# Window attention with a gate, one core: scores of four quarters added up in one PSUM bank

## The chip, the core and the metric

The kernel runs on one core of a Trainium2 chip. A core has a matrix engine (TensorE, PE in the profile), a vector engine (VectorE, DVE), a scalar engine (ScalarE, ACT), GpSimd (POOL) and a queue engine (SyncE, SP) which here issues nearly all of the loads. Each engine executes its own instructions in order, and engines wait for each other through semaphores. Matmul results go to PSUM, which has eight banks of 128 partitions by 512 float32 numbers. The metric is the device time of one execution in microseconds (us); lower is better.

## The reference

A single decode step for two sequences. Everything is float32.

```python
xn = _layernorm(x)                                   # x: 2 x 1 x 512
# attention over the last W = 4096 positions of a cache of 32768
q = (xn @ wq)                                        # 32 query heads of 128, 8 key/value heads
k = k_cache[:, :, Sk - W:, :]; v = v_cache[:, :, Sk - W:, :]
p = softmax(einsum("bhqd,bhkd->bhqk", q, k) * Dh ** -0.5)
s = einsum("bhqk,bhkd->bhqd", p, v).reshape(B, 1, 4096) @ wo
# gated MLP on the same xn
z = gelu(xn @ w_in); z1 = z[..., :896]; z2 = _layernorm(z[..., 896:])
y = (z1 * (w_sp * z2 + b_sp)) @ w_out
out = x + s * silu(y)
```

The weights and the two windows of the caches amount to 89.4 MB, each byte of which is read once.

## The kernel before

**Units.** The attention is cut into eight units. A unit holds two key/value heads of one sequence, so eight query heads. Its keys are one load of 4096 KB and its values another: partition p holds 64 consecutive positions of one of the two heads (64 partitions for each head), J = 64 positions of 128 numbers each.

**Loads.** All large tensors pass through a pool `ring` of four slots of 32 KB for each partition. SP issues the loads in one order: `win`, `wout`, two halves of `wq`, then `k0`, `v0`, `k1`, `v1`, ... `k7`, `v7`, then `wo` in pieces of 16, 8, 4, 2, 1 and 1 blocks. The fifth load takes the first slot again, and so on. So the load of `k` of unit u+2 waits on SP until the last reader of `k` of unit u has ended, and the load of `v` of unit u+2 until `values` of unit u has ended.

**Scores.** A unit's 64 positions are done in NCH = 4 quarters of JC = 16 positions. For quarter m:

- `turn(u, m)`: VectorE transposes the 128x2048 block of keys in 32x32 squares into `kt`, of which there are two buffers.
- `shares(u, m)`: four matmuls of 128x32 weights (the queries) and 512 columns, one for each quarter of the 128 numbers of a head, into one PSUM bank `sh`. They give four shares of each score, which lie in different partitions. ScalarE copies the bank to `shs`.
- `add_shares(u, m)`: one matmul with the 0/1 matrix `add_dq` (128x128) adds the four shares. Its output is the m-th of the four banks of the tile `s`. Partition 32g + 16a + 4h of it holds the scores of query h of key head a with the keys of partition group g; the other rows are zero.

**Softmax.** `row_max` takes the maximum over 1536 columns (three banks) and then over 512 columns (the last). `share_max` masks it (`t` twice, `mg`), sums over partitions by a matmul (`mo`), takes a maximum (`mx`) and makes the bias `nb`. `probs` are two exponentials on ScalarE, each over 1024 of the 2048 columns (even and odd ones), which also add up the sums `l`. `probs_t` transposes `p` on VectorE in two halves of 1024 columns into `pT`. `weights` sums `l` over partitions by a matmul and makes the factors `wd` on VectorE.

**Values.** `values` is 16 matmuls of 128x32 weights and 512 columns into the bank `acc`, with four groups of columns of the array side by side. `scale_out` scales `acc` on ScalarE in four pieces into `o`, and `collect` (four matmuls) puts the rows of interest into a bank `col` for each sequence. After the last unit of a sequence `gather` reduces it into `oT`. At the end `part` (56 records) and `so` multiply by `wo`, and two vector operations apply the gate.

**Order.** All the engines' instructions keep the order in which the program writes them (`InOrder`). In one turn of the loop over units, with `prev` the unit before: exponentials of `prev`; turn and shares of quarter 0 of u; both halves of `probs_t` and `weights` of `prev`; `add_shares` 0; `values` of `prev`; then for the quarters 1, 2 and 3 turn, shares, `add_shares`; then `scale_out` and `collect` of `prev`; the maxima of u.

**PSUM.** `s` takes four banks, and `sh`, `acc`, `mo` and `col` one each: all eight.

Of the kernel before, what the change touches and what calls it, by code (L numbers as in the profile page):

```python
# [9 lines left out]
F32 = mybir.dt.float32  # L10
AF = mybir.ActivationFunctionType
ALU = mybir.AluOpType
AX = mybir.AxisListType

P = 128
HQ, DH = 32, 128
G = 4
# [4 lines left out]
def ap(t, offset, dims):  # L22

    return bass.AP(tensor=t.tensor, offset=t.offset + offset, ap=[list(t.ap[0])] + [list(d) for d in dims])
# [18 lines left out]
def kernel(  # L43
# [14 lines left out]
    pe, dve, act, sp = (InOrder(tc, e) for e in (nc.tensor, nc.vector, nc.scalar, nc.sync))  # L58
    B, _, D = x.shape
    _, HKV, SK, _ = k_cache.shape  # L60
    W = min(4096, max(256, SK // 4))
    REP = HQ // HKV
# [7 lines left out]
    J = 2 * W // P  # L70
    JC = 512 // 32
    NCH = J // JC
    SLOT = J * DH

    ring = ctx.enter_context(tc.tile_pool(name="ring", bufs=4))
    cst = ctx.enter_context(tc.tile_pool(name="cst", bufs=1))
    sb = ctx.enter_context(tc.tile_pool(name="sb", bufs=2))
# [5 lines left out]
    def const(name, *shape):  # L83
        return cst.tile([P, *shape], F32, tag=name, name=name)

    def bank(name, tag):
        return ps.tile([P, 512], F32, tag=tag, name=name)


    xs = cst.tile([B, D], F32, tag="xs", name="xs")  # L90
# [8 lines left out]
    wqt = []  # L99
# [29 lines left out]
    nc.gpsimd.memset(hT, 0.0)  # L129
    x4 = const("x4", DC)  # L130
    nc.gpsimd.memset(x4, 0.0)
    add_dq = const("add_dq", G, 32)
    nc.gpsimd.memset(add_dq, 0.0)
    sel = const("sel", 35)
    nc.gpsimd.memset(sel, 0.0)
# [33 lines left out]
    same = const("same", G, 32)  # L169
    dve.tensor_copy(same, ap(rowm, 0, [[0, G], [1, 32]]))  # L170
    same = same.rearrange("p g c -> p (g c)")
    heads = const("heads", 16, 8)
    dve.tensor_copy(heads, ap(rowm, 0, [[0, 16], [4, 8]]))
    heads = heads.rearrange("p x r -> p (x r)")
    diag = const("diag", 4)
    dve.tensor_reduce(diag, rowm.rearrange("p (j r) -> p j r", j=4), axis=AX.X, op=ALU.add)
    dve.tensor_reduce(sel[:, 3:35:4], rowm.rearrange("p (j r) -> p r j", j=4), axis=AX.X, op=ALU.add)
    for a in range(2):
        dve.tensor_copy(add_dq[:, :, 16 * a : 16 * a + 16 : 4], rowm[:, 16 * a : 16 * a + 16].rearrange("p (g h) -> p g h", g=G))
    add_dq = add_dq.rearrange("p g r -> p (g r)")  # L180
    am = const("am", 2)
    dve.tensor_reduce(am, ap(rowm, 0, [[16, 2], [4, REP]]), axis=AX.X, op=ALU.add)
    negm = const("negm", 2)
    dve.tensor_scalar(negm, am, -1.0, BIG, op0=ALU.add, op1=ALU.mult)


    FQ = FH // G
# [56 lines left out]
    for j in range(FT):  # L244
        g = j % G
# [10 lines left out]
    dve.tensor_mul(gate, gate, y)  # L256


    pq = ps.tile([P, 2, 512], F32, tag="s", name="q_ps")
    for k in range(KT):  # L260
        for r in range(2):
            for g in range(G):
                c = (r * G + g) * 512
                pe.matmul(
                    pq[32 * g : 32 * g + 32, r, :], xnT[:, k, :], wqt[k // 2][:, k % 2, c : c + 512],
                    start=(k == 0), stop=(k == KT - 1),
                )
    qT = sb.tile([P, 1024], F32, tag="qT", name="qT", bufs=1)
    dve.transpose(qT, pq.rearrange("p r c -> p (r c)"))
    qm = const("qm", 2 * B * 64)  # L270
    for gs in range(G):
        for b in range(B):
# [16 lines left out]

    def turn(u, m):  # L290

        u.kt[m] = sb.tile([P, JC, DH], F32, tag="kt", name=f"kt{u.n}_{m}")
        dve.transpose(
            u.kt[m].rearrange("p j d -> p (j d)"), u.k[:, JC * m : JC * m + JC, :].rearrange("p j d -> p (j d)")
        )

    def shares(u, m):

        u.sh = bank(f"sh{u.n}_{m}", "sh")
        for dq in range(4):  # L300
            pe.matmul(
                u.sh[32 * dq : 32 * dq + 32, :], q_of(u, dq), u.kt[m][:, :, 32 * dq : 32 * dq + 32],
                start=True, stop=True,
            )
        u.shs[m] = sb.tile([P, 512], F32, tag="shs", name=f"shs{u.n}_{m}")
        act.activation(u.shs[m], u.sh, AF.Copy)

    def add_shares(u, m):
        if m == 0:
            u.s = ps.tile([P, NCH, 512], F32, tag="s", name=f"s{u.n}")  # L310
            u.m4 = sb.tile([P, 2, 2], F32, tag="m4", name=f"m4_{u.n}")
        pe.matmul(u.s[:, m, :], add_dq, u.shs[m], start=True, stop=True)

    def row_max(u, i, c0, c1):
        dve.tensor_reduce(
            u.m4[:, i, :], ap(u.s, 512 * c0, [[1, 2], [2, 256 * (c1 - c0)]]), axis=AX.X, op=ALU.max
        )

    def share_max(u):
        t = sb.tile([P, 2], F32, tag="t", name=f"t{u.n}")  # L320
        dve.tensor_scalar_mul(t, u.m4[:, :, 0], am[:, 0:1])
        dve.scalar_tensor_tensor(t, u.m4[:, :, 1], am[:, 1:2], t, op0=ALU.mult, op1=ALU.add)
        mg = sb.tile([P, 2, G], F32, tag="mg", name=f"mg{u.n}")
        dve.tensor_mul(mg, ap(t, 0, [[1, 2], [0, G]]), ap(grpm, 0, [[0, 2], [1, G]]))
        u.mo = bank(f"mo{u.n}", "mo")
        pe.matmul(u.mo[:, : 2 * G], same, mg.rearrange("p a g -> p (a g)"), start=True, stop=True)
        mx = sb.tile([P, 1], F32, tag="mx", name=f"mx{u.n}")
        dve.reduce_max(mx, u.mo[:, : 2 * G], axis=AX.X)
        u.nb = sb.tile([P, 2], F32, tag="nb", name=f"nb{u.n}")
        dve.scalar_tensor_tensor(u.nb, ap(mx, 0, [[0, 2]]), -SCALE, negm, op0=ALU.mult, op1=ALU.add)  # L330

    def probs(u):

        u.p = sb.tile([P, J, 32], F32, tag="p", name=f"p{u.n}", bufs=1)
        u.l = sb.tile([P, 2], F32, tag="l", name=f"l{u.n}")
        for a in range(2):
            act.activation(
                ap(u.p, a, [[2, J * 16]]), ap(u.s, a, [[2, J * 16]]), AF.Exp,
                bias=u.nb[:, a : a + 1], scale=SCALE, accum_out=u.l[:, a : a + 1],
            )  # L340

    def probs_t(u, half):
        if half == 0:
            u.pT = sb.tile([P, J, 32], F32, tag="pT", name=f"pT{u.n}", bufs=1)
        h = slice(J // 2 * half, J // 2 * (half + 1))
        dve.transpose(u.pT[:, h].rearrange("p j r -> p (j r)"), u.p[:, h].rearrange("p j k -> p (j k)"))

    def weights(u):
        pe.matmul(u.mo[:, 2 * G : 2 * G + 2], heads, u.l, start=True, stop=True)
        l = sb.tile([P, 1], F32, tag="ls", name=f"ls{u.n}")  # L350
        dve.reduce_sum(l, u.mo[:, 2 * G : 2 * G + 2], axis=AX.X)
        dve.reciprocal(l, l)
        u.wd = sb.tile([P, 4], F32, tag="wd", name=f"wd{u.n}")
        dve.tensor_scalar_mul(u.wd, diag, l)

    def values(u):
        u.acc = bank(f"acc{u.n}", "acc")
        NQ = J // 4
        for q in range(NQ):
            c = q % G  # L360
            pe.matmul(
                u.acc[32 * c : 32 * c + 32, :], ap(u.pT, 4 * q * 32, [[4, 32]]),
                u.v[:, 4 * q : 4 * q + 4, :].rearrange("p j d -> p (j d)"), start=(q < G), stop=(q >= NQ - G),
            )

    def scale_out(u):
        u.o = sb.tile([P, 4, DH], F32, tag="o", name=f"o{u.n}")
        for jj in range(4):
            act.activation(
                u.o[:, jj, :], u.acc[:, jj * DH : (jj + 1) * DH], AF.Copy, scale=u.wd[:, jj : jj + 1]  # L370
            )
# [3 lines left out]
    def collect(u):  # L375
        if u.w == 0:
            col[u.b] = bank(f"col{u.b}", "col")[:, : 4 * 32].rearrange("p (j d) -> p j d", j=4)
        for e in range(4):
            pe.matmul(
                col[u.b][32 * u.w : 32 * u.w + 32], sel[:, 3 - e : 35 - e], u.o[:, :, 32 * e : 32 * e + 32],  # L380
                start=(e == 0), stop=(e == 3),
            )
# [28 lines left out]
                for b in range(B):  # L411
                    sp.dma_start(x4[16 * b : P : 32, :], by_group(x, b, 0, DC))

    def finish(u):
        scale_out(u)
        collect(u)

    prev = None
    for u in units:
        if prev is not None:  # L420
            probs(prev)
        turn(u, 0)
        shares(u, 0)
        if prev is not None:
            probs_t(prev, 0)
            probs_t(prev, 1)
            weights(prev)
        add_shares(u, 0)
        if prev is not None:
            values(prev)  # L430
        for m in range(1, NCH):
            turn(u, m)
            shares(u, m)
            add_shares(u, m)
        if prev is not None:
            finish(prev)
        row_max(u, 0, 0, NCH - 1)
        row_max(u, 1, NCH - 1, NCH)
        share_max(u)
        if prev is not None:  # L440
            gather(prev)
        prev = u
    probs(prev)
    probs_t(prev, 0)
    probs_t(prev, 1)
    weights(prev)
    values(prev)
    finish(prev)
    gather(prev)


# [49 lines left out]
```

## Time and profile before

| | us |
|---|---|
| three runs | 260.6, 262.8, 265.55 |
| their median | 262.8 |
| the profiled execution, whole time | 261.21 |
| its span, from the first to the last instruction | 259.4 |

| engine | busy us | share of the span |
|---|---|---|
| TensorE | 161.7 | 62% |
| VectorE | 137.0 | 53% |
| ScalarE | 54.8 | 21% |

The page of the profile shows the busy time of each engine, the span in 40 equal slices (each digit a busy share in tenths), the queues of the transfers, the chain of work that ended last, and the costliest groups of instructions. Nearly all instructions stand under line 37, because a helper records them; the names of tiles tell them apart. A float32 matmul shows as two records, so 16 matmuls are "x32". The granted clock is the share of TensorE's full clock that the chip gave in a stretch. The span and all durations are of one execution; the whole time of that execution is 1.8 us more than its span.

### The profile page before, as it was taken

Reading aid. Unit: us, or ns where it says so; the run is one execution under the profiler, and the core shown is the slowest. Engines: PE = TensorE matmul, PEld = TensorE weight load, DVE = VectorE, ACT = ScalarE, POOL = GpSimd, SP = SyncE. Lnnn points to the kernel's source line nnn. Section 1 sums busy time; section 2 is a strip of 40 time slices with the busy share of each in tenths; the row PEclk is TensorE's granted clock in tenths of the full one; section 3 lists DMA queues with packets and bytes.
Section 4 is the critical chain, followed back from the end, with each engine's and each line's share of the span. In section 5 each row is a group of like instructions: output and inputs, shape, how many; then the busy total and the mean of one; then the engine's idle time right before and its main releaser. Section 6 shows DMA issues by size and latency. Waiting matters only on the chain.

```text
span 259.4 us, 2310 instructions
## 1 busy us (share of the span) xinstructions
PE 161.7 (62%) x898; PEld 49.2 (19%) x898; DVE 137.0 (53%) x191; ACT 54.8 (21%) x109; POOL 2.5 (1%) x13
## 2 busy tenths in 40 slices
PE   0261894285297559637872976497368729763893
PEld 0111221011121122122220212121222112121131
DVE  3234115861893486369618933873696189435000
ACT  4004100011301240233033012401330330123100
POOL 3000000000000000000000000000000000000000
PEclk9996579569569967995998599779959995997798
DMA  7999999999999997999499769958994998591000
GB/s 284 418 466 409 450 428 414 450 429 419 450 424 422 450 419 344 384 424 421 149 414 470 328 237 407 404 248 323 467 419 167 404 424 386 197 396 56 0 3 1
DMA packets 3794, 89.54 MB, mean 345 GB/s; under 512 B 438, under 2 KB 454, under 8 KB 840
## 3 DMA queue, kind: packets, MB, share of 16 engines
q1 hardware_dynamic: 3768, 89.40, 81.6%
q8 instruction: 7, 0.11, 0.2%
q10 hardware_dynamic: 16, 0.01, 0.0%
q14 instruction: 3, 0.02, 0.0%
HBM read 89.40 MB, written 0.00 MB: 345 GB/s over the span
## 4 chain that ended last, share of the span: by engine, by line
PE 53%; DVE 18%; DMA 16%; ACT 9%; issue 3%; ACTq 0%
PE s L37 17%; PE sh L37 16%; PE acc L37 14%; DMA k<-in_A_k_cache_dram 12%; ACT shs L37 7%; DVE m L37 7%; DVE kt L37 7%; DMA win<-in_B_w_in_dram 4%; PE part L37 2%; PE z L37 2%; DVE t L37 1%; PE mo L37 1%; ACT p L37 1%; DVE mg L37 1%; DVE mx L37 1%
## 5 line engine op out<-in xcount | busy, mean ns | idle before, releaser
L37 DVE STREAM_TRANSPOSE kt<-k 128x2048 f32<-128x2048 f32 x32 | 72.8, 2297 | 19.8 <-PE sh L37 19.1
L37 PE MATMUL s<-shs,add_dq 128*128 128x512 f32 x64 | 43.6, 768 | 21.3 <-ACT shs L37 21.3
L37 PE MATMUL sh<-kt,qbd 128*32 128x512 f32 x256 | 41.6, 729 | 24.3 <-DVE kt L37 24.3
L37 ACT ACTIVATE shs<-sh 128x512 f32<-128x512 f32 x32 | 19.1, 597 | 125.2 <-PE sh L37 125.2
L37 DVE TENSOR_REDUCE m<-s 128x2 f32<-128x1536 f32 (+1 forms) x16 | 18.8, 1219 | 42.9 <-PE s L37 42.9
L37 PE MATMUL acc<-v,pT 128*32 128x512 f32 x256 | 35.8, 709 | 0.7 <-DVE pT L37 0.7
L37 ACT ACTIVATE p<-s,nb 128x1024 f32<-128x1024 f32 x16 | 18.5, 1168 | 34.8 <-DVE nb L37 34.8
L37 DVE STREAM_TRANSPOSE pT<-p 128x1024 f32<-128x1024 f32 x16 | 19.0, 1224 | 4.4 <-ACT p L37 4.3
L37 PEld LDWEIGHTS s<-shs,add_dq 128*128 128x128 f32 x64 | 11.1, 218 | 46.2 <-ACT shs L37 43.7
L37 PEld LDWEIGHTS acc<-v,pT 128*32 128x32 f32 x256 | 9.3, 146 | 30.8 <-issue 30.0
L37 PE MATMUL mo<-mg,same 128*128 128x8 f32 x16 | 3.3, 280 | 18.4 <-DVE mg L37 18.4
L37 PEld LDWEIGHTS sh<-kt,qbd 128*32 128x32 f32 x256 | 6.2, 117 | 42.9 <-issue 37.8
L37 ACT ACTIVATE o<-acc,wd 128x128 f32<-128x128 f32 x32 | 9.1, 374 | 7.3 <-PE acc L37 7.3
L37 PE MATMUL q_ps<-wq,xnT 128*32 128x512 f32 x64 | 9.3, 734 | 0.6 <-DMA wq<-in_A_wq_dram 0.6
L37 PE MATMUL col<-o,sel 128*32 128x128 f32 x64 | 8.5, 275 | 1.3 <-ACT o L37 1.3
L37 PEld LDWEIGHTS col<-o,sel 128*32 128x32 f32 x64 | 6.3, 109 | 7.5 <-ACT o L37 6.7
L37 PE MATMUL z<-win,xnT 128*32 128x448 f32 x32 | 4.5, 723 | 4.6 <-DMA win<-in_B_w_in_dram 4.6
L37 PEld LDWEIGHTS mo<-l,heads 128*128 128x128 f32 x16 | 4.0, 311 | 14.6 <-issue 11.6
L37 PEld LDWEIGHTS mo<-mg,same 128*128 128x128 f32 x16 | 2.6, 203 | 21.1 <-DVE mg L37 21.1
L37 PE MATMUL mo<-l,heads 128*128 128x2 f32 x16 | 4.7, 363 | 2.9 <-ACT p L37 2.9
L37 PE MATMUL part<-wo,oT 128*32 128x512 f32 x56 | 6.2, 593 | 0.4 <-issue 0.4
L37 PE MATMUL y<-wout,hT 128*32 128x512 f32 x14 | 3.6, 1059 | 4.0 <-DVE hT L37 4.0
(99 smaller groups left out, 57.3 us busy)
## 6 DMA issues: line engine op xcount, KB each, us to landing
k<-in_A_k_cache_dram SPq DMA_DIRECT2D x8, 4096.0 KB, 21.6
v<-in_A_v_cache_dram SPq DMA_DIRECT2D x8, 4096.0 KB, 13.1
wq<-in_A_wq_dram SPq DMA_DIRECT2D x2, 4096.0 KB, 29.7
wo<-in_A_wo_dram SPq DMA_DIRECT2D x1, 4096.0 KB
win<-in_B_w_in_dram SPq DMA_DIRECT2D x1, 3584.0 KB
wo<-in_A_wo_dram SPq DMA_DIRECT2D x1, 2048.0 KB
wout<-in_B_w_out_dram SPq DMA_DIRECT2D x1, 1792.0 KB, 15.1
wo<-in_A_wo_dram SPq DMA_DIRECT2D x1, 1024.0 KB
```

The lines of the kernel that those rows point to most:

```text
L37: return self.tc.keep_in_program_order(call(*args, **kwargs))
```

## The change

The four quarters of a unit's scores go to one bank instead of four. The 0/1 matrix `add_dq` becomes 131 columns wide; for quarter m the matmul takes the 128 columns that begin at 3 - m, so that quarter m's rows land on rows that the other quarters leave at zero, and the four matmuls accumulate in the bank. Row 4r + m of a group of 32 then belongs to quarter m and to r = 4a + h.

- `row_max` is gone; the maximum `m2` is one reduction over 512 columns, the two masking operations `t` are gone, and `mg` multiplies by a prepared mask `spot`. The sum over partitions is two accumulating matmuls (`same_r`) instead of one.
- The two exponentials take 256 columns each, `probs_t` is one transpose of 512 columns.
- `values` takes its 32 weight columns from one position `j` of `pT` and the positions j, j+16, j+32, j+48 of `v`: 16 matmuls as before.
- PSUM: two banks each for `s`, `sh` and `acc`, one each for `mo` and `col`. `kt` has three buffers, `p` and `pT` two.
- The order in a turn of the loop: exponentials, transpose, weights and `values` of `prev` come first. Then the quarters of u, in which `add_shares` of quarter m - 1 stands behind `shares` of quarter m; `scale_out` of `prev` stands in quarter 1, `collect` of `prev` ahead of the last `add_shares`.
- Some vector operations are added to the set-up (`rowr`, `same_r`, `spot`), and `qT` is transposed in two halves. The loads and their order are the same.

```diff
+    BANKS = {"s": 2, "sh": 2, "acc": 2, "mo": 1, "col": 1}
...
-    add_dq = const("add_dq", G, 32)
+    add_dq = const("add_dq", NCH - 1 + P)
...
+    spot = const("spot", 2, G, NCH)
+    for a in range(2):
+        dve.tensor_mul(spot[:, a], ap(grpm, 0, [[1, G], [0, NCH]]), ap(diag, 0, [[0, G], [1, NCH]]))
+        dve.tensor_scalar_mul(spot[:, a], spot[:, a], am[:, a : a + 1])
...
-    dve.transpose(qT, pq.rearrange("p r c -> p (r c)"))
+    for r in range(2):
+        dve.transpose(qT[:, 512 * r : 512 * r + 512], pq[r])
...
-        pe.matmul(u.s[:, m, :], add_dq, u.shs[m], start=True, stop=True)
+        pe.matmul(u.s, add_dq[:, NCH - 1 - m : NCH - 1 - m + P], u.shs[m], start=(m == 0), stop=(m == NCH - 1))
...
-    def row_max(u, i, c0, c1):
-        dve.tensor_reduce(
-            u.m4[:, i, :], ap(u.s, 512 * c0, [[1, 2], [2, 256 * (c1 - c0)]]), axis=AX.X, op=ALU.max
-        )
...
-        dve.tensor_scalar_mul(t, u.m4[:, :, 0], am[:, 0:1])
-        dve.scalar_tensor_tensor(t, u.m4[:, :, 1], am[:, 1:2], t, op0=ALU.mult, op1=ALU.add)
+        dve.tensor_reduce(m2, ap(u.s, 0, [[1, 2], [2, 256]]), axis=AX.X, op=ALU.max)
...
-        pe.matmul(u.mo[:, : 2 * G], same, mg.rearrange("p a g -> p (a g)"), start=True, stop=True)
+        for a in range(2):
+            pe.matmul(u.mo[:, : G * NCH], same_r, mg[:, a], start=(a == 0), stop=(a == 1))
...
-                ap(u.p, a, [[2, J * 16]]), ap(u.s, a, [[2, J * 16]]), AF.Exp,
+                ap(u.p, a, [[2, 256]]), ap(u.s, a, [[2, 256]]), AF.Exp,
...
-                u.acc[32 * c : 32 * c + 32, :], ap(u.pT, 4 * q * 32, [[4, 32]]),
-                u.v[:, 4 * q : 4 * q + 4, :].rearrange("p j d -> p (j d)"), start=(q < G), stop=(q >= NQ - G),
+                u.acc[32 * c : 32 * c + 32, :], u.pT[:, j, :], u.v[:, j : J : JC, :],
+                start=(j < G), stop=(j >= JC - G),
...
         if prev is not None:
             probs(prev)
-        turn(u, 0)
-        shares(u, 0)
-        if prev is not None:
-            probs_t(prev, 0)
-            probs_t(prev, 1)
+            probs_t(prev)
             weights(prev)
-        add_shares(u, 0)
-        if prev is not None:
             values(prev)
-        for m in range(1, NCH):
+        for m in range(NCH):
             turn(u, m)
             shares(u, m)
-            add_shares(u, m)
+            if m > 0:
+                add_shares(u, m - 1)
+            if m == 1 and prev is not None:
+                scale_out(prev)
         if prev is not None:
-            finish(prev)
-        row_max(u, 0, 0, NCH - 1)
-        row_max(u, 1, NCH - 1, NCH)
+            collect(prev)
+        add_shares(u, NCH - 1)
         share_max(u)
```

More of the change, by code (lines that the diff above doesn't have):

```diff
@@ L86, in bank @@
     def bank(name, tag):
-        return ps.tile([P, 512], F32, tag=tag, name=name)
+        return ps.tile([P, 512], F32, tag=tag, name=name, bufs=BANKS[tag])
     xs = cst.tile([B, D], F32, tag="xs", name="xs")
@@ L171 @@
     same = same.rearrange("p g c -> p (g c)")
[L172 to L177, printed above, removed]
+    rowr = const("rowr", 8)
+    dve.tensor_reduce(rowr, rowm.rearrange("p (r m) -> p r m", m=NCH), axis=AX.X, op=ALU.add)
+    same_r = const("same_r", G, 8, NCH)
+    dve.tensor_copy(same_r, ap(rowr, 0, [[0, G], [1, 8], [0, NCH]]))
+    same_r = same_r.rearrange("p g r m -> p (g r m)")
+    diag = const("diag", NCH)
+    dve.tensor_reduce(diag, rowm.rearrange("p (r m) -> p m r", m=NCH), axis=AX.X, op=ALU.add)
+    dve.tensor_copy(sel[:, 3:35:4], rowr)
     for a in range(2):
-        dve.tensor_copy(add_dq[:, :, 16 * a : 16 * a + 16 : 4], rowm[:, 16 * a : 16 * a + 16].rearrange("p (g h) -> p g h", g=G))
-    add_dq = add_dq.rearrange("p g r -> p (g r)")
+        dve.tensor_copy(
+            ap(add_dq, NCH - 1 + 16 * a, [[32, G], [4, REP]]),
+            rowm[:, 16 * a : 16 * a + 16].rearrange("p (g h) -> p g h", g=G),
+        )
     am = const("am", 2)
-    dve.tensor_reduce(am, ap(rowm, 0, [[16, 2], [4, REP]]), axis=AX.X, op=ALU.add)
+    dve.tensor_reduce(am, rowm.rearrange("p (a x) -> p a x", a=2), axis=AX.X, op=ALU.add)
     negm = const("negm", 2)
     dve.tensor_scalar(negm, am, -1.0, BIG, op0=ALU.add, op1=ALU.mult)
+    spot = const("spot", 2, G, NCH)
+    for a in range(2):
+        dve.tensor_mul(spot[:, a], ap(grpm, 0, [[1, G], [0, NCH]]), ap(diag, 0, [[0, G], [1, NCH]]))
+        dve.tensor_scalar_mul(spot[:, a], spot[:, a], am[:, a : a + 1])
     FQ = FH // G
@@ L256 @@
     dve.tensor_mul(gate, gate, y)
-    pq = ps.tile([P, 2, 512], F32, tag="s", name="q_ps")
+    pq = [bank(f"q_ps{r}", "s") for r in range(2)]
     for k in range(KT):
@@ L264 @@
                 pe.matmul(
-                    pq[32 * g : 32 * g + 32, r, :], xnT[:, k, :], wqt[k // 2][:, k % 2, c : c + 512],
+                    pq[r][32 * g : 32 * g + 32, :], xnT[:, k, :], wqt[k // 2][:, k % 2, c : c + 512],
                     start=(k == 0), stop=(k == KT - 1),
@@ L290, in turn @@
     def turn(u, m):
-        u.kt[m] = sb.tile([P, JC, DH], F32, tag="kt", name=f"kt{u.n}_{m}")
+        u.kt[m] = sb.tile([P, JC, DH], F32, tag="kt", name=f"kt{u.n}_{m}", bufs=3)
         dve.transpose(
@@ L309, in add_shares @@
         if m == 0:
-            u.s = ps.tile([P, NCH, 512], F32, tag="s", name=f"s{u.n}")
-            u.m4 = sb.tile([P, 2, 2], F32, tag="m4", name=f"m4_{u.n}")
-        pe.matmul(u.s[:, m, :], add_dq, u.shs[m], start=True, stop=True)
-    def row_max(u, i, c0, c1):
-        dve.tensor_reduce(
-            u.m4[:, i, :], ap(u.s, 512 * c0, [[1, 2], [2, 256 * (c1 - c0)]]), axis=AX.X, op=ALU.max
-        )
-    def share_max(u):
-        t = sb.tile([P, 2], F32, tag="t", name=f"t{u.n}")
-        dve.tensor_scalar_mul(t, u.m4[:, :, 0], am[:, 0:1])
-        dve.scalar_tensor_tensor(t, u.m4[:, :, 1], am[:, 1:2], t, op0=ALU.mult, op1=ALU.add)
-        mg = sb.tile([P, 2, G], F32, tag="mg", name=f"mg{u.n}")
-        dve.tensor_mul(mg, ap(t, 0, [[1, 2], [0, G]]), ap(grpm, 0, [[0, 2], [1, G]]))
+            u.s = bank(f"s{u.n}", "s")
+        pe.matmul(u.s, add_dq[:, NCH - 1 - m : NCH - 1 - m + P], u.shs[m], start=(m == 0), stop=(m == NCH - 1))
+    def share_max(u):
+        m2 = sb.tile([P, 2], F32, tag="m2", name=f"m2_{u.n}")
+        dve.tensor_reduce(m2, ap(u.s, 0, [[1, 2], [2, 256]]), axis=AX.X, op=ALU.max)
+        mg = sb.tile([P, 2, G * NCH], F32, tag="mg", name=f"mg{u.n}")
+        dve.tensor_mul(mg, ap(m2, 0, [[1, 2], [0, G * NCH]]), spot.rearrange("p a g m -> p a (g m)"))
         u.mo = bank(f"mo{u.n}", "mo")
-        pe.matmul(u.mo[:, : 2 * G], same, mg.rearrange("p a g -> p (a g)"), start=True, stop=True)
+        for a in range(2):
+            pe.matmul(u.mo[:, : G * NCH], same_r, mg[:, a], start=(a == 0), stop=(a == 1))
         mx = sb.tile([P, 1], F32, tag="mx", name=f"mx{u.n}")
-        dve.reduce_max(mx, u.mo[:, : 2 * G], axis=AX.X)
+        dve.reduce_max(mx, u.mo[:, : G * NCH], axis=AX.X)
         u.nb = sb.tile([P, 2], F32, tag="nb", name=f"nb{u.n}")
@@ L332, in probs @@
     def probs(u):
-        u.p = sb.tile([P, J, 32], F32, tag="p", name=f"p{u.n}", bufs=1)
+        u.p = sb.tile([P, 512], F32, tag="p", name=f"p{u.n}")
         u.l = sb.tile([P, 2], F32, tag="l", name=f"l{u.n}")
@@ L337, in probs, with probs_t @@
             act.activation(
-                ap(u.p, a, [[2, J * 16]]), ap(u.s, a, [[2, J * 16]]), AF.Exp,
+                ap(u.p, a, [[2, 256]]), ap(u.s, a, [[2, 256]]), AF.Exp,
                 bias=u.nb[:, a : a + 1], scale=SCALE, accum_out=u.l[:, a : a + 1],
             )
[L342 to L346, printed above, removed]
+    def probs_t(u):
+        u.pT = sb.tile([P, JC, 32], F32, tag="pT", name=f"pT{u.n}")
+        dve.transpose(u.pT.rearrange("p j r -> p (j r)"), u.p)
     def weights(u):
-        pe.matmul(u.mo[:, 2 * G : 2 * G + 2], heads, u.l, start=True, stop=True)
+        pe.matmul(u.mo[:, 32:34], same_r, u.l, start=True, stop=True)
         l = sb.tile([P, 1], F32, tag="ls", name=f"ls{u.n}")
-        dve.reduce_sum(l, u.mo[:, 2 * G : 2 * G + 2], axis=AX.X)
+        dve.reduce_sum(l, u.mo[:, 32:34], axis=AX.X)
         dve.reciprocal(l, l)
-        u.wd = sb.tile([P, 4], F32, tag="wd", name=f"wd{u.n}")
+        u.wd = sb.tile([P, NCH], F32, tag="wd", name=f"wd{u.n}")
         dve.tensor_scalar_mul(u.wd, diag, l)
@@ L357, in values @@
         u.acc = bank(f"acc{u.n}", "acc")
-        NQ = J // 4
-        for q in range(NQ):
-            c = q % G
+        for j in range(JC):
+            c = j % G
             pe.matmul(
-                u.acc[32 * c : 32 * c + 32, :], ap(u.pT, 4 * q * 32, [[4, 32]]),
-                u.v[:, 4 * q : 4 * q + 4, :].rearrange("p j d -> p (j d)"), start=(q < G), stop=(q >= NQ - G),
+                u.acc[32 * c : 32 * c + 32, :], u.pT[:, j, :], u.v[:, j : J : JC, :],
+                start=(j < G), stop=(j >= JC - G),
             )
@@ L412 @@
                     sp.dma_start(x4[16 * b : P : 32, :], by_group(x, b, 0, DC))
-    def finish(u):
-        scale_out(u)
-        collect(u)
     prev = None
@@ L443 @@
     probs(prev)
-    probs_t(prev, 0)
-    probs_t(prev, 1)
+    probs_t(prev)
     weights(prev)
     values(prev)
-    finish(prev)
+    scale_out(prev)
+    collect(prev)
     gather(prev)
```

## The prediction, made blind

> **What bounds the kernel now.** I read the page first: the span and the row of the transfers in 40 slices.
>
> ```profile
> span 259.4 us, 2310 instructions
> DMA  7999999999999997999499769958994998591000
> ```
>
> The transfers are at nine tenths or more up to the 15th slice, with one exception at the start, and from the 16th on there are holes. So the first 97 us are set by the memory, and later something makes the transfers wait. Next came busy time by stretches: start and end, length, busy time of PE, weight loads, DVE, ACT and POOL, then the granted clock, the transfers' share and GB/s.
>
> ```profile
> 2.00:97.00 95.00, 51.26 (x267) 14.93 (x268) 46.62 (x89) 18.72 (x33) 1.01 (x3) 0.80 1.00 429
> 115.00:235.00 120.00, 81.87 (x422) 24.71 (x422) 76.06 (x83) 29.08 (x60) 0.00 (x0) 0.86 0.83 347
> 122.00:124.00 2.00, 2.00 (x9) 0.41 (x12) 2.00 (x2) 0.00 (x0) 0.00 (x0) 0.50 1.14 492
> 124.00:126.00 2.00, 2.00 (x24) 0.60 (x20) 1.53 (x1) 0.00 (x0) 0.00 (x0) 0.98 0.04 8
> 126.00:128.00 2.00, 1.87 (x20) 0.37 (x12) 0.05 (x1) 0.00 (x0) 0.00 (x0) 1.00 0.00 0
> ```
>
> With its queue full, the core takes 429 GB/s; in the second half the mean is 347, because in each unit there are some 4 us without a byte, as from 124 to 128. Who holds the transfers back is in the waits of SP's queue (total us, times, longest):
>
> ```profile
> SPq L37 <- PE acc L37: 139.7, 7, 20.3
> ```
>
> SP stands up to 20.3 us ahead of a load of `v` until `values` has given the slot back, and the load of `k` is queued behind it. Compute is the bound of the later units. Its period is in the chain of work (start, us, what):
>
> ```profile
> 115.64 2.23 DVE kt L37
> 117.88 0.14 issue
> 118.01 1.97 PE sh L37 x8
> 120.06 0.61 ACT shs L37
> 120.71 2.08 PE s L37 x2
> 122.79 4.23 PE acc L37 x32
> ...
> 132.68 1.04 PE sh L37 x8
> 133.81 0.61 ACT shs L37
> 134.46 1.14 PE s L37 x2
> 135.62 2.37 DVE m L37 x2
> 138.01 0.24 DVE t L37
> 138.28 0.23 DVE t L37
> 138.53 0.18 DVE mg L37
> 138.75 0.40 PE mo L37 x2
> 139.18 0.18 DVE mx L37
> 139.38 0.16 DVE nb L37
> 139.54 2.23 DVE kt L37
> ```
>
> From one bias `nb` to the next it is 139.54 - 115.64 = 23.90 us, and every engine waits in turn: each quarter goes through shares, copy and sum without anything beside it, and the maxima come at the end. Matmuls begin at half the clock (`sh` 1.97 against 1.04, `s` 2.08 against 1.14) and run at the full one from about 124 on.
>
> **The loads as the new floor.** The loads themselves are not changed.
>
> ```profile
> k<-in_A_k_cache_dram SPq DMA_DIRECT2D x8, 4096.0 KB, 21.6
> 16.74 30.25 DMA k<-in_A_k_cache_dram
> ```
>
> A load is 4096 KB = 4.194 MB, so a unit's two are 8.39 MB, at 429 GB/s 19.55 us. The first `k` lands at 16.74 + 30.25 = 46.99. If the queue never runs dry, the eighth lands 7 x 19.55 later, at 183.8. [...]
>
> Does the queue stay full? It takes slots in order. The load of `k` for unit u+2 waits for the last turn of unit u, some 9 us after `k` of u landed, and its own time in the queue comes after three more loads, 29 us after that landing. The load of `v` for u+2 waits for `values` of u, worked out below at 24 us after the landing at most, against 39. Some 15 us of slack are left, so nothing that SP waits for is late.
>
> **Compute, part by part.** Durations for the remaining terms:
>
> ```profile
> 121.03 4.50 DVE L37 STREAM_TRANSPOSE kt<-k 128x2048 f32<-128x2048 f32 x2
> L37 DVE TENSOR_REDUCE m<-s 128x2 f32<-128x512 f32 x8 | 5.4, 680 | 0.0
> ```
>
> ```profile
> 235.23 2.37 ACT p L37 x4
> 237.62 1.26 DVE pT L37
> 238.93 5.97 PE acc L37 x32
> 244.92 1.15 ACT o L37 x4
> 246.12 1.06 PE col L37 x8
> 247.18 0.43 issue
> 247.61 6.25 PE part L37 x56
> ```
>
> ```profile
> 241.50 0.19 PEld L37 LDWEIGHTS acc<-v,pT 128*32 128x32 f32 x4 [0.66 <-issue]
> 242.35 0.19 PEld L37 LDWEIGHTS acc<-v,pT 128*32 128x32 f32 x4 [0.66 <-issue]
> ```
>
> Turns: two back to back take 4.50, so four take 9.0, and with the third `kt` buffer nothing stops them: the fourth needs only `shares` of quarter 0. With 0.14 for the issue and a few hundredths to start, `sh` of quarter 3 can begin 9.2 us after `k` lands. Matmuls from there: the new order puts `sh` 3, `s` 2, `col`, `s` 3 on PE, 1.04 + 1.14 + 1.06 + 1.14 = 4.4; the copies of 0.61 lie beside them. That cover needs the two `sh` banks; without it each copy costs its 0.61. The three earlier `sh` and two `s` fit into the turns when `values` is done in time.
>
> Maximum: from the end of the last `s` (134.46 + 1.14 = 135.60) to the start of the next work (139.54) was 3.94. The reduction goes from 2.37 to 0.70 (the 680 ns row and a hand-over), the two `t` go (138.01 to 138.53, 0.52), the second `mo` matmul adds between 0 and 0.40; I take 0.3, since the two follow each other without a wait. That leaves 2.05. So `nb` comes 9.2 + 4.4 + 2.05 = 15.6 after the landing.
>
> Exponentials and transpose: 2.37 for two of 1024 columns. For two of 256 the ends are a quarter, 0.59, and two copies of 512 columns, 2 x 0.61 = 1.22; I take 1.05, near the upper end, since a copy or a reduction of few elements still costs 0.16 to 0.18 here. Half of `pT` took 1.26 and a turn of twice its columns 2.23 to 2.25, so 512 columns take about 0.76. Together 1.8. `weights` lies beside `values`.
>
> `values`: the same 16 matmuls, 4.23 when mostly warm. Cold, four records pass each 0.85 us (241.50 to 242.35), so 32 take 6.8. I see no reason for another price in the strided columns of `v`; if there were one, it would stand under the turns of the next unit, as long as `sh` 0 isn't late by more than some 2 us.
>
> Set-up: the added vector operations come before the wait for `win` at 12 us, where DVE has nothing else; without that they would be 1 us.
>
> Compute alone would have the period 1.8 + `values` 4.2 to 6.8 + four `sh`, four `s` and `col` (4 x 1.04 + 4 x 1.14 + 1.06 = 9.8) + 2.05 = 17.8 to 20.4 us, about 19 in the middle. That is under the 19.55 of the loads, though not by much. So the bound moves from the round of the engines to the loads, and what each unit saves is 23.9 - 19.55 = 4.35 us, not the 6 that compute alone gives.
>
> **Sum.** The last `k` lands at 183.8; `nb` at 199.4; `values` begins at 201.2; from there to the end nothing is changed: before, 238.93 to 259.4, 20.5 us. Span 221.7. Are the last weights there? `v7` and 8.39 MB of `wo` take 29.3 us after 183.8, so the last block lands at 213.1; `part` would begin at 201.2 + 8.7 = 209.9 and need its last four blocks, landed at about 211, at 215. The transfers end some 4 us ahead of need. The profiled execution took 261.21, 1.8 over its span, so 223.5 here; the median of the three runs, 262.8, is 1.006 times the profiled one, hence 225.
>
> **Rivals.** *Compute stays the bound.* The loads are faster than matmuls that begin cold in every unit: at the upper end of 20.4 us and a first `nb` at about 64 (`k0` 47 and 17 for a cold start), the last `nb` is at 206.8, the span 229.1, the median 232. For it: PE would work 14 to 17 us of 20 on its own queue, and the clock falls in gaps like the one between `s` and `values`. Against it: that gap shrinks, and half of the quarters then run warm. Chance 0.19.
>
> *The loads don't sustain 429.* If the 347 of the second half were what the memory gives and the holes its manner, a unit takes 24.2 us, the last `k` lands at 216, the span is 254 and the median 257: within 2%, which is about what a measurement of this kernel can tell from no change, as its three runs lie 1.9% apart. For it speaks only the mean; against it the rows of 8 and 0 GB/s in which SP waits for `values`. [...] Chance 0.04.
>
> *The clock doesn't come back.* [...] Then the period is 1.8 + 6.8 + 4 x 1.97 + 4 x 2.08 + 2.1 + 2.05 = 29 us, and the median near 295. It decides from the point where the period is over 25.5 (last `nb` at 242, 2% slower), that is with about 70% of the matmul work cold. Against it: in every unit so far the clock came back after some 6 us of work with similar waits in it. Chance 0.03. [...]
>
> **How the numbers follow.** The forecast, loads as the bound, has 0.72; 0.02 is left for less than its range. Its own range is 219 to 228: below by warm `values` at the end (5.97 to 4.23), exponentials and transpose at their lower ends (0.5) and loads 1% faster; above by late cold quarters. The whole range reaches up to the first rival, with 0.4 us more a unit for hand-overs that the sums leave out, 235, and to 218 below for the scatter of the runs. Faster by over 2%: 0.72 + 0.19 + 0.02 = 0.93. Within: 0.04. Slower: 0.03.
>
> **What the profile would show.** Right: transfers at nine tenths from the start to some 210 us without holes; DVE's first `kt` of each unit waiting for `k` by DMA, units about 19.6 us apart; about 16 us from that `kt` to `nb`; SP no longer waiting 20 us for `acc` with an empty queue. Wrong: first `kt` of a unit held by DVE's own order with `k` long there, holes in the transfers, `sh` near 2 us in all quarters, or `acc` well over 6.8.

## The result and the profile after

| | before | after |
|---|---|---|
| median, us (4 runs each) | 263.9 (260.6 to 265.55) | 222.31 (221.41 to 222.86) |
| profiled execution, us | 261.21 | 222.86 |
| its span, us | 259.4 | 221.1 |
| mean granted clock | 0.838 | 0.865 |

The ratio is 0.849, with a 95% interval from 0.841 to 0.857; it compares fast executions alone and leaves out two slow ones of the kernel before (265.01 and 265.55), so it is not the quotient of the medians. The forecast was 225 for the median and 221.7 for the span.

First the same rows of the page as before, and then busy time by stretches (the last two columns are the transfers' share and GB/s).

```profile
span 221.1 us, 2319 instructions
DMA  7999999999999999999999999999999999999910
```

```profile
2.00:97.00 95.00, 58.98 (x335) 17.29 (x336) 46.66 (x91) 18.78 (x40) 1.01 (x3) 0.86 1.00 428
97.00:205.00 108.00, 87.80 (x470) 27.99 (x471) 59.04 (x69) 23.21 (x64) 0.00 (x0) 0.86 1.00 429
```

The holes are gone. The transfers run at 429 GB/s in the second half and at 428 in the first, so 89.4 MB flow almost without a pause to about 210 us. In the waits of all engines (total, times, longest), and of SP's queue:

```profile
DVE kt L37 <- DMA k<-in_A_k_cache_dram: 13.9, 8, 1.8
PE sh L37 <- DVE kt L37: 11.4, 8, 5.8
```

```profile
SPq L37 <- PE acc L37: 88.5, 7, 13.6
```

VectorE now waits in each unit up to 1.8 us for keys to land. SP still stands up to 13.6 us ahead of a load of `v`. But the load it issues then has another one in front of it in the queue, so nothing dries up: beside SP's 88.5 us of waits here the transfers' share is 1.00 from 97 to 205 us, where the kernel before, with 139.7, had 0.83 from 115 to 235. The long wait says nothing by itself here; the holes in the transfers say it.

The chain of work through the last two units (start, us, what):

```profile
163.36 4.52 DVE kt L37 x2
167.88 0.14 issue
168.02 1.06 PE sh L37 x8
169.08 1.06 PE s L37 x2
...
174.53 0.99 PE col L37 x8
175.52 1.07 PE s L37 x2
176.59 0.02 issue
176.61 0.70 DVE m L37
...
177.58 0.63 PE mo L37 x4
...
178.70 1.03 ACT p L37 x4
...
179.76 0.72 DVE pT L37
...
180.52 6.02 PE acc L37 x32
...
199.94 6.61 PE acc L37 x32
```

Before 163.36 the chain is a load of `k`; from there on it is mostly TensorE's queue, with no copy between shares and sums. The two `values` take 6.02 and 6.61: the mean granted clock was 0.60 over the first (180.52 to 186.54) and 0.55 over the second (199.94 to 206.55), against 1.00 and 3.64 us in the first unit. In the last unit two paths end together. Its turns begin at 182.78, straight after the landing of `k7`, and take 8.89 us, to 191.67; the last `sh` can begin 0.14 later and begins at 191.82, and TensorE's queue comes free for it at 191.75. So the landing of the last keys fixes this chain as much as the queue does.

Of the 38.3 us between the two spans, 5.4 lie ahead of the first bias `nb` (67.71 before, 62.32 after), 31.7 in the seven spacings from there to the last `nb` (234.97 and 197.87), and 1.2 behind it.

### The profile page after: what moved, and what is told of

The parts are those of the page before. It is cut to its first block, busy times and chain, and to the rows that moved or that the text cites. A ratio compares the mean times of both kernels' runs of the same rounds, so it can differ in the third digit from the quotient of the medians.

```text
span 221.1 us, 2319 instructions
## 1 busy us (share of the span) xinstructions
PE 156.8 (71%) x914; PEld 49.4 (22%) x914; DVE 107.1 (48%) x165; ACT 43.8 (20%) x109; POOL 2.5 (1%) x13
## 4 chain that ended last, share of the span: by engine, by line
DMA 59%; PE 21%; DVE 13%; issue 4%; ACT 2%; ACTq 0%
DMA k<-in_A_k_cache_dram 53%; DVE kt L37 11%; PE acc L37 6%; DMA win<-in_B_w_in_dram 5%; PE s L37 4%; PE sh L37 3%; PE part L37 3%; PE z L37 3%; PE col L37 1%; ACT p L37 1%; DVE pT L37 1%; DVE m L37 1%; PE so L37 1%; PE mo L37 1%; ACT o L37 1%
## 5 line engine op out<-in xcount | busy, mean ns | idle before, releaser
L37 PE MATMUL acc<-v,pT 128*32 128x512 f32 x256 | 43.1, 835 | 2.1 <-DVE ls L37 1.6
L37 PE MATMUL sh<-kt,qbd 128*32 128x512 f32 x256 | 35.7, 631 | 12.4 <-DVE kt L37 11.4
L37 PE MATMUL s<-shs,add_dq 128*128 128x512 f32 x64 | 36.7, 659 | 0.0
L37 DVE TENSOR_REDUCE m<-s 128x2 f32<-128x512 f32 x8 | 5.5, 692 | 35.3 <-PE s L37 35.3
L37 ACT ACTIVATE p<-s,nb 128x256 f32<-128x256 f32 x16 | 7.5, 481 | 35.0 <-DVE nb L37 35.0
L37 PE MATMUL mo<-l,same_r 128*128 128x2 f32 x16 | 3.8, 310 | 12.6 <-ACT p L37 12.6
L37 PE MATMUL mo<-mg,same_r 128*128 128x16 f32 x32 | 5.0, 268 | 8.1 <-DVE mg L37 8.1
L37 DVE STREAM_TRANSPOSE pT<-p 128x512 f32<-128x512 f32 x8 | 5.7, 711 | 9.0 <-ACT p L37 9.0
L37 PEld LDWEIGHTS mo<-mg,same_r 128*128 128x128 f32 x32 | 4.2, 190 | 14.7 <-DVE mg L37 14.7
L37 PEld LDWEIGHTS mo<-l,same_r 128*128 128x128 f32 x16 | 3.2, 247 | 13.4 <-ACT p L37 13.4
```

Of the source, the lines that this page charges most:

```text
L37: return self.tc.keep_in_program_order(call(*args, **kwargs))
```

## The experiments

Each was timed beside the kernel before on the same chip, where that had medians of 260.8 to 261.1.

**Are the loads the floor? Fewer loads, before and after.** Both kernels got the same edit:

```diff
     for u in units:
-        u.k = load_unit(k_cache, u.n, "k")
-        u.v = load_unit(v_cache, u.n, "v")
+        if u.n < 2:
+            u.k = load_unit(k_cache, u.n, "k")
+            u.v = load_unit(v_cache, u.n, "v")
+        else:
+            u.k, u.v = units[u.n % 2].k, units[u.n % 2].v
```

> The kernel before with the same loads left out (units 2 to 7 work on the caches of units 0 and 1). Compute is the bound before: units 23.9 us apart as ever, 261 to 265. Rival, the memory gave only 347 GB/s and set the pace: the time falls by more than 10 us.

The kernel before took 261.6 us (ratio 1.003, 1.000 to 1.006) with 50 MB less to load. Its page shows the transfers standing still for half of the span:

```profile
DMA  7999999999920000000000000000000870591000
```

So compute was the whole bound before, and the rival that took 347 GB/s for the memory's rate falls.

> The changed kernel with the caches of units 2 to 7 not loaded: those units work again on the keys and values of unit 0 or 1, so 50 MB of loads are left out and the output is another. Loads as the floor of the changed kernel, with compute just under it: units come 17.6 to 19.3 us apart instead of 19.43 (1.9 for exponentials and transpose, values 4.2 to 6.0, 9.4 of shares and sums, 2.1 for the maximum), median 213 to 221. Rival, compute has been the bound all along and its 19.4 us only look like those of the loads: 222, units 19.4 apart.

The changed kernel took 217.44 us. In its instructions in order of time, the first and the last `nb`:

```profile
62.00 0.16 DVE L37 SCALAR_TENSOR_TENSOR nb<-mx,negm 128x2 f32<-128x2 f32 x1
...
193.12 0.16 DVE L37 SCALAR_TENSOR_TENSOR nb<-mx,negm 128x2 f32<-128x2 f32 x1
```

Seven units in 131.12 us are 18.73 each: inside the expected 17.6 to 19.3, and the rival's 19.4 is out. With all loads the same rows stand at 62.32 and 197.87, 19.36 each, and from the second unit on 19.43. The loads are the floor, but compute lies only 0.7 us a unit under it.

**How much slack is that? More work on the chain.** The maximum is done two, three and four times:

```diff
-        dve.tensor_reduce(m2, ap(u.s, 0, [[1, 2], [2, 256]]), axis=AX.X, op=ALU.max)
+        for _ in range(3):
+            dve.tensor_reduce(m2, ap(u.s, 0, [[1, 2], [2, 256]]), axis=AX.X, op=ALU.max)
```

> The changed kernel with the maximum over the 512 columns done three times instead of once: 2 x 0.70 = 1.4 us more a unit on the chain to nb. Loads as the floor with some 0.8 us of slack a unit: 1.4 at the last unit and 0.6 at the seven others, 226 to 229. No slack (compute as the bound): 8 x 1.4, 233 to 234. Slack over 1.4: 223.5 to 224.5.

Three times: 230.54 us, between "0.8 us of slack" (226 to 229) and "no slack" (233 to 234), with 20.5 us a unit. The transfers still run at 429 GB/s from 97 to 205 us, but from the third unit on the first turn no longer waits for its keys: compute is the bound here.

> The changed kernel with the maximum done twice (0.70 us more a unit on the chain). If what is added simply adds to compute's own 18.7: 19.4, level with the loads, median 222.5 to 224.5. If compute, once it is the bound, falls in step with the clock's own rhythm (20.49 with two more maxima is 6 times 3.41 us; before, 23.9 is 7 times): 20.5 a unit, 229 to 231.

Twice: 223.13 us. The units are 18.7 to 20.4 apart, 19.57 in the mean; 0.7 us more a unit costs 0.8 us in all. That is the slack, measured.

> The changed kernel with the maximum done four times (2.1 us more a unit). Simple addition to compute's own 18.7: 20.8, median 231 to 234. In step with a rhythm of 3.41 us: again 20.5 (230 to 232) or two units together in 13 steps, 22.2 a unit (241 to 244).

Four times: 232.37 us. That is inside what simple addition gives (231 to 234) and 0.4 above what the rhythm of 3.41 us was to give (230 to 232). The units come 21.17, 21.12, 20.80, 20.64, 20.55, 20.51 and 20.50 us apart: the mean of 20.76 is that of simple addition, the last units run at the 20.5 of the rhythm. The time alone doesn't decide between the two.

**Is it the gap in the softmax that lets the clock fall?** Two groups of matmuls that nobody reads:

```diff
+    def keep_warm(u):
+        d = bank(f"w{u.n}", "sh")
+        for dq in range(4):
+            pe.matmul(
+                d[32 * dq : 32 * dq + 32, :], q_of(u, dq), u.kt[NCH - 1][:, :, 32 * dq : 32 * dq + 32],
+                start=True, stop=True,
+            )
...
+        keep_warm(u)
         for a in range(2):
             pe.matmul(u.mo[:, : G * NCH], same_r, mg[:, a], start=(a == 0), stop=(a == 1))
+        keep_warm(u)
```

> The changed kernel with two further groups of four matmuls a unit (as in shares, into a bank that nobody reads), one behind the last add_shares and one behind the mo matmuls, to keep TensorE at work while the maximum and the exponentials run. If the clock falls because of that gap, values takes 4.3 us instead of 6 to 6.6. Loads as the floor: units stay 19.4 apart, only the end gains some 2 us, median 219.5 to 221. Rival, compute is the bound: units 17.6 to 18 us apart, median 208 to 212. Third case, the gap isn't what lets the clock fall: 222 to 224.

219.95 us (219.86 to 221.76). The chain of its last unit:

```profile
194.87 1.06 PE s L37 x2
195.92 1.00 PE w L37 x8
...
199.88 3.69 PE acc L37 x32
```

`values` takes 3.69 instead of 6.61, and the mean granted clock is 0.937 instead of 0.865. Yet the units stay 19.4 us apart in the mean, and the last `nb` comes at 197.80 against 197.87. All the time made inside the units goes into waiting for keys; only what lies behind the last unit's keys counts. If compute had been the floor, 17.6 to 18 us a unit should have shown.

> The kernel with the further groups of matmuls and, as in after_few_loads, without the loads of the caches of units 2 to 7 (another output). The falling clock costs compute 2 us a unit: with values at 3.7 a unit is 3.7 + 8.9 of shares and sums + 4.0 from the last sum to the next values = 16.6 to 17 us, last nb near 180, median 200 to 204. Rival, the clock costs only the end and something else holds the units at 18.7: 215.

With the loads left out as well, 210.42 us, neither of the two. In the later units the spacing is 17.52, not 16.6 to 17:

```profile
120.34 0.23 DVE wd L37
120.57 4.42 DVE kt L37 x2
124.99 0.14 issue
125.12 1.07 PE sh L37 x8
```

With TensorE warm (`values` takes 3.64 us from the third unit to the seventh) the chain goes through VectorE: the transpose of `pT` and the three operations of `weights` stand ahead of the turns, and the second `sh` waits for the second turn. The expectation's sum for compute had no such term. It was also too low for the whole time because the second unit still came 21.07 after the first.

**Which half of the change does it?** One kernel has the new scores, banks and `kt` buffers with the loop of before; the other has the loop of after, three `kt` buffers and the four banks of before.

```diff
# new_scores_old_order: the loop of before around the changed functions
         turn(u, 0)
         shares(u, 0)
         if prev is not None:
             probs_t(prev)
             weights(prev)
         add_shares(u, 0)
         if prev is not None:
             values(prev)
         for m in range(1, NCH):
             turn(u, m)
             shares(u, m)
             add_shares(u, m)
...
# old_scores_new_order: the changed loop around the functions of before
             probs_t(prev, 0)
             probs_t(prev, 1)
             weights(prev)
             values(prev)
         for m in range(NCH):
             turn(u, m)
             shares(u, m)
             if m > 0:
                 add_shares(u, m - 1)
```

> The new scores (one bank, one 512-column maximum, exponentials and transpose of a quarter of the size, two banks each, three kt buffers) in the order of before. The two parts work only together: the exponentials and the transpose lay beside the turn there, so a unit loses only the maximum's 1.67 and the two t's 0.52 and gains 0.2 for mo: 23.9 to 21.9 us, with 2 each at the first unit and at the end, median 244 to 248. Rival, the scores do it alone: 222 to 226.

> The scores of before (four banks, 2048 columns of maximum, exponentials and transpose, one sh and one acc bank) in the new order, with three kt buffers. The full-size exponentials (2.37), half a transpose (1.26) and maximum (3.94 to nb) now stand in the chain: 2.37 + 1.26 + values 4.2 to 6.8 + 9.4 + 0.65 for the copy that one sh bank shows + 3.94 = 21.8 to 24.4 us a unit, median 250 to 266, so little or nothing. Rival, the order does it alone: 222 to 230.

| us (ratio to before) | order of before | order of after |
|---|---|---|
| scores of before | 260.8 | 257.48 (0.987, 0.979 to 0.996) |
| scores of after | 244.42 (0.935, 0.929 to 0.942) | 222.31 (0.849, 0.841 to 0.857) |

(The changed kernel's ratio is from its own comparison, beside 263.9.) The scores alone bring 16 us, the order alone some 3 (1 to 5 by its interval), both together 38.5. The chain of the kernel with old scores in the new order shows why the order alone is worth so little:

```profile
182.71 2.37 ACT p L37 x4
185.08 0.02 issue
185.11 1.26 DVE pT L37
186.36 0.04 issue
186.41 6.01 PE acc L37 x32
```

The new order takes the turn and three of the four copies of the shares off the chain (the first copy still shows, as there is one `sh` bank here) and puts the exponentials and the transpose on it. At 2048 columns these cost 3.6 us, and `values` takes 6.01 instead of 4.23 (the mean granted clock is 0.802 against 0.838), so hardly anything is left of the gain (the units are 23.8 us apart); at 512 columns the two cost 1.75. The second banks of `s` and `acc` and the second buffers of `p` and `pT` were not tried alone.

**The second bank for `sh`.** `"sh": 2` becomes `"sh": 1`.

> The changed kernel with one bank for sh instead of two. As the prediction said it, each copy then costs its 0.61: 2.4 us a unit, of which some 0.8 is slack, median 233 to 236. Rival, add_shares of the quarter before lies between two shares and hides all copies but the first: 0.65 a unit, 222 to 224.

229.37 us (226.1 to 231.18, ratio to the kernel before 0.870, 0.860 to 0.879): between the two. The chain of one unit:

```profile
128.13 0.91 PE sh L37 x8
129.04 0.02 issue
129.07 0.02 ACTq L37
129.08 0.04 issue
129.13 0.60 ACT shs L37
129.73 0.04 issue
129.78 1.06 PE sh L37 x8
130.84 1.06 PE s L37 x2
131.90 1.00 PE sh L37 x8
```

Only the first copy shows; the `s` of the quarter before hides the others, as the rival said. But 0.65 us more on the chain is about all the slack, and `values` takes 6.3 to 6.6 us from the fourth unit on, where the first took 3.64, so the last five are 20.1 to 20.4 apart. The transfers don't slow down (430 GB/s from 140 to 205 us); it is compute that falls behind them. The first turn waits less and less for its keys, 1.94, 1.23 and 0.35 us in the fifth to the seventh unit, and in the last not at all.

**The third `kt` buffer.** `bufs=3` becomes `bufs=2`.

> The changed kernel with two kt buffers instead of three. The third turn then waits for the shares of quarter 0, which end about 4.9 us after the keys have landed, where two turns end at 4.5: some 0.4 us a unit, inside the slack of the loads, 222 to 223. Rival, the third buffer is what lets the turns run through: 225 or more.

221.96 us: no difference, and not the 225 of the rival.

**A version beyond both.** The keys of each unit come in two loads, in the kernel with the further matmuls:

```diff
-        sp.dma_start(t, src)
+        H = SLOT // 2 if name == "k" else SLOT
+        for c in range(0, SLOT, H):
+            src = bass.AP(tensor=first.tensor, offset=first.offset + c, ap=[[SLOT, P // 2], [SK * DH, 2], [1, H]])
+            sp.dma_start(t[:, c : c + H], src)
```

> The kernel with the further groups of matmuls, and each unit's keys loaded in two halves of 2048 KB, so that two turns can run before the second half lands. The last unit's chain from the landing of its keys to nb shortens until TensorE's queue is the limit (values of unit 6 end at about 184.2, 9.4 more to the last sum instead of 195.9): 2 us less, median 217 to 218.5. Rival, the last wo blocks (landing near 211) set the end already: 219 to 220.

218.74 us (218.59 to 218.89, ratio to the kernel before 0.838, 0.834 to 0.841), between the expectation and the rival, and the fastest of the study with all loads. The last `nb` comes 3.9 us earlier, at 193.94, but the end only 1.3:

```profile
187.79 22.29 DMA wo<-in_A_wo_dram
210.08 0.04 issue
210.12 1.11 PE part L37 x8
```

The last weights now set the end, as the rival said, so what is left on top of the loads is the work on the last blocks, some 7 us.

## Why the prediction was right, point by point

- **The bound before** was compute: shown by the kernel before with fewer loads, 261.6.
- **The loads as the new floor.** A unit was to take 19.55 us and took 19.43; the last keys were to land at 183.8, and their first turn began, straight after the landing, at 182.78. The 429 GB/s on which the sum rested, from 2 to 97 us of the kernel before, came again from 97 to 205 us here.
- **The queue never runs dry.** Some 15 us of slack were forecast. The load of `v7` is issued at 166.47, as `values` of the sixth unit ends, and its turn in the queue comes when `k7` has landed, at about 182.8: 16 us.
- **From the keys to `nb`**: 15.6 forecast, 182.78 to 198.04 = 15.26 measured. Maximum 0.70, `mo` with its second matmul 0.63 instead of 0.40 (0.3 more were taken, 0.23 it is), exponentials 1.03 (1.05), transpose 0.72 (0.76).
- **The end**: the forecast left it unchanged from the start of `values` on, 20.5 us. It took 221.1 - 199.94 = 21.2, because `values` was colder, 6.61 instead of 5.97 (mean granted clock 0.55). This is the one term of the sum that clearly went the other way, and after_warm, where it took 3.69, shows its cause. Small errors partly cancelled: 1.0 us early at the keys, 0.3 on the way to `nb`, 0.7 late at the end, so the span came 0.6 early.
- **From the span to the median**: the 1.8 us over the span held (222.86 - 221.1), but the factor of 1.006 did not. It came from three runs of the kernel before, one of them at 265.55; here the median lies 0.5 us under the profiled execution. That makes some 2 of the 2.7 us between 225 and 222.31.
- **Compute alone, 17.8 to 20.4 and about 19**: 18.73 measured. So the first rival, compute still the bound, came within 0.7 us a unit. The forecast held because the clock was cold in about the share of the work that the middle assumed (in after_few_loads `values` took 5.06 to 6.46 us from the second unit on; the middle of 4.2 and 6.8 is 5.5), and nothing in the sum could tell how large that share would be: this much was luck. A little more on the chain, as with one `sh` bank or a maximum done three times, and that rival is what one gets.
- **Wrong among the covers**: "without it each copy costs its 0.61", said of the two `sh` banks. Only one of four shows, 0.65 us a unit. The third `kt` buffer, named as what lets the turns run through, does nothing for the time.
- **The clock that doesn't come back** had no case: the fourth `sh` of every unit took 1.06 or 1.07 us, where at half the clock one took 1.93 or 1.94. From the second unit on the granted clock fell to 0.50 once a unit, five times between the last `s` and `values` (at 82.97, 120.52, 141.00, 178.54 and 199.02 us) and twice just after `values` had begun (0.64 and 0.40 us, at 103.45 and 161.48); 3.41 or 6.83 us later it was back at 1.00. In after_warm, from the second unit on, only the third `values` (5.33 us) and one `sh` with the `s` behind it (1.94 and 1.75, at 167.75) took clearly longer than the others (3.69, 1.07 and 1.13 at most). That a kernel of this kind could stay at half the clock throughout, 29 us a unit, was the author's estimate; no run shows it.

## What to carry to other kernels

Work out the period of each bound for itself, compute with its clock cold and warm, transfers at the rate of a stretch where their queue is full: the new period is the larger one, and the gain ends there (here 4.5 us a unit, where compute would have given 5.2). A smaller operation and another order can be worth little each and much together, when the order puts on the chain just what the other makes small. Where two bounds lie within a microsecond, take away the loads in one experiment and add a known piece of work in another; together they measure the slack.

## What was not expected of the hardware

- Small matmuls in the gap did not hold the clock. From the last sum to `values` it is 3.9 us (176.59 to 180.52 in the seventh unit); with two short `mo` groups in between, TensorE stands still for no more than about 1.6 us at a time. Yet in seven units of eight `values` took 5.0 to 6.6 us, at a mean granted clock of 0.55 to 0.72, with 0.85 us for four records while cold; in the first it took 3.64, at 1.00. Two groups of full size in the gap (after_warm) kept it at 3.64 to 3.69 in seven units of eight.
- The granted clock changed on a grid. In the traces of the kernel before and of the changed one (21 and 19 changes) every change lies a whole number of steps of 3.41 us from every other change of the same trace. In the last unit of the changed kernel the clock falls at 199.02, and in the step of 3.41 us before that TensorE was busy for 1.0 us; it comes back at 205.85, two steps later. In its first unit the gap (60.4 to 64.4) lies across a step, at 62.49, and the clock stays full, with 1.99 us busy in the step before and 1.89 in the step after. That it matters where a gap lies on the grid was the author's estimate from these two units; it was not shown, since the steps ahead of the seven falls from 82.97 to 199.02 were busy for 0.83 to 2.06 us. At which share of busy time it falls, these runs don't tell.
- Where compute set the pace and the clock fell in unit after unit, the period came close to a whole number of these steps, for one unit or for two together. With the maximum done three times, the clock repeats from 62.58 us on, 6.83 us at half and 13.65 full, 20.48 together or 6 steps (start and end, length, busy times, then granted clock, transfers' share and GB/s):

```profile
171.81:185.46 13.65, 10.57 (x64) 3.42 (x56) 6.88 (x8) 3.53 (x9) 0.00 (x0) 1.00 1.01 435
185.46:192.29 6.83, 5.71 (x27) 1.69 (x30) 5.82 (x7) 0.91 (x4) 0.00 (x0) 0.50 0.98 422
```

  The kernel before runs at 23.9 us a unit, 7 x 3.41, and the old scores in the new order come to 23.9 too; two units of the new scores in the old order take 44.3, 13 x 3.41. The maximum done three and four times, 0.7 us of work apart, both come to 20.5, and with four times `values` grows shorter from unit to unit, from 5.99 to 5.03 us, until it fits:

```profile
188.09 0.16 DVE L37 SCALAR_TENSOR_TENSOR nb<-mx,negm 128x2 f32<-128x2 f32 x1
208.59 0.16 DVE L37 SCALAR_TENSOR_TENSOR nb<-mx,negm 128x2 f32<-128x2 f32 x1
```

  With fewer loads, short and long units alternate (19.20 and 18.14, 19.30 and 18.19), two of them 37.3 to 37.5, 11 x 3.41. With one `sh` bank the last four spacings are 20.13, 20.31, 20.39 and 20.44, still under 6 steps (20.48). In after_warm_few_loads, where `values` takes 3.64 us from the third unit to the seventh, the period is 17.52, no whole number of steps. That a unit is drawn into step because its cold stretch ends on the grid is argued from these rows; no run moved the one against the other. What it does to an estimate the runs show: the second 0.7 us added to a unit's chain cost (230.54 - 223.13) / 8 = 0.93 us a unit, the third (232.37 - 230.54) / 8 = 0.23.
